# Sink attention's row sums, inverted by another engine

## The chip, the cores and the metric

The program runs on one core of a Trainium2 chip. A core has five engines that each work through a list of their own, in order: TensorE (PE in the profile, with its weight loads as PEld), VectorE (DVE), ScalarE (ACT), GpSimd (POOL) and SyncE (SP, which only starts DMAs here). They meet through semaphores. The metric is the device time of one execution in microseconds.

## What is computed

Attention over 768 positions, for 2 batches and 8 heads of 64 columns, in which each query sees the 4 first positions (the sinks) and a window of 128 positions; then a feed-forward block with a gated convolution; then a mixture of four attention experts. The change lies in the division by the row sums of the first attention:

```python
scores = np.where(keep, scores, -1000000000.0)
scores = scores - np.max(scores, axis=-1, keepdims=True)
a = np.exp(scores)
a = a / (np.sum(a, axis=-1, keepdims=True) + 1e-09)
return np.matmul(a, v).astype(np.float32)
```

## The kernel before, in words

The first attention (span 0 to about 150 us) works on tiles of 128 queries: 6 tiles for each of 2 batches, 12 in all. Each tile runs in 4 steps, one for each pair of heads. In a step `a1_S` multiplies queries by keys (TensorE, L500 for the first batch and L487 for the second), subtracts from the mask and takes the row maximum (VectorE, L502), and takes exponentials whose row sums land in two columns of a small tile `su` (ScalarE, L505, each with a second instruction that reads the sum out). After its 4 steps a tile has `su`, 128 queries by 8 heads. `a1_r` adds the epsilon (L512) and inverts (L513), in place. `a1_rT` lets TensorE transpose `su` to 8 by 128 (L530); the result `rT` is copied from PSUM by ScalarE or VectorE (L517, L519), written to DRAM (L534) and read back spread over the partitions as `R` (L541). `x_norm` multiplies the attention's output by it (L545).

Around this, TensorE transposes the exponentials (`a1_T`, L561) and multiplies them by the values (`a1_V`, L603). GpSimd collects the sinks' columns into `G` (`a1_gather`, L576 for each pair, L578 for each tile), computes two slices of `vsr`, the low part of the sinks' values, in the first batch (L308), and from about 60 us, when the feed-forward block starts to overlap with the second batch, does a multiplication by a convolution weight (L792, tile `ht`) and the low part of the gate (L820, tile `g`) for each step of that block. VectorE and ScalarE also decode the 64-bit weights in the background (L355 to L365, tile `f64u`; L429, L523, L525).

Everything is written in Python in the order in which each engine is to do it (`manual_schedule`). The order comes from time steps: each part of a tile has a lag in steps (`LAGS`), and within a step the string `ORD1` sets the sequence. In it `a1.gather`, `a1.S` and `a1.r` (the second batch) stand in the middle and `a0.r` (the first batch) stands near the end. `a1_r` runs one step behind its tile's last `a1_S`; `a1_rT` one or more parts later. An engine never passes over an instruction that waits: whatever stands behind it in that engine's list waits too.

Of the kernel before, what the change touches and what calls it, by code (L numbers as in the profile page):

```python
# [8 lines left out]
F32 = mybir.dt.float32  # L9
# [6 lines left out]
ALU = mybir.AluOpType  # L16
# [3 lines left out]
B, H, S, D = 2, 8, 768, 64  # L20
P = 128
# [19 lines left out]
EPS = 1e-9  # L41
# [6 lines left out]
def run_phases(phases):  # L48


    at = {}
    for k, (o, n, stages, rate) in enumerate(phases):
        for m, (lag, fn, *g) in enumerate(stages):
            for i in range(n):
                first = i - i % g[0] if g else i
                at.setdefault(o + math.floor(lag + first * rate), []).append((k, m, i, fn))
    for t in sorted(at):
        for _, _, i, fn in sorted(at[t], key=lambda c: c[:3]):
            fn(i)
# [30 lines left out]
class Kernel:  # L90
# [57 lines left out]
    def consts(self, pool):  # L148
        nc = self.nc
        self.words = pool.tile([P, 4], I32, name="words")  # L150
        self.ident = pool.tile([P, P], F32, name="ident")
        self.causal = pool.tile([P, 4 * P], F32, name="causal")
        self.cw = pool.tile([P, 3 * NF], F32, name="cw")
        self.flag = pool.tile([P, 1], I32, name="flag")
        self.lims = pool.tile([P, 2], F32, name="lims")
        self.guard = pool.tile([P, 2 * NF + 1], F32, name="guard")
        self.ones = pool.tile([P, 1], F32, name="ones")
        self.below = pool.tile([P, 1], F32, name="below")
        self.nsink, self.window = self.lims[:, 0:1], self.lims[:, 1:2]
        self.m0 = pool.tile([P, P], F32, name="m0")  # L160
        self.m1 = pool.tile([P, 2 * P], F32, name="m1")
        self.mEO = [pool.tile([P, 2, KW], F32, name=f"m{i}x") for i in range(2)]
# [346 lines left out]

    def a1_r(self, b, qt):  # L510
        r = self.a1s[(b, qt)]
        self.nc.vector.tensor_scalar(r, r, EPS, None, op0=ALU.add)  # L512
        self.nc.vector.reciprocal(r, r)  # L513

    def copy(self, e, dst, src):
        if e == "a":
# [661 lines left out]
    def program(self, general):  # L1178
        tc, nc = self.tc, self.nc
        tg = "g" if general else "f"  # L1180
        self.x, self.y, self.v2, self.lg, self.rw = {}, {}, {}, {}, {}
        self.ks, self.qs = {}, {}
        self.qkv, self.wraw, self.a2P, self.a2PT, self.a2z = {}, {}, {}, {}, {}
        with ExitStack() as ctx:
            def op(name, bufs=1, **kw):
                g = tc.tile_pool(name=name + tg, bufs=bufs, reuse_waits="tile", **kw)
                return g, g.__enter__()

            self.halves = not general
            gSm, self.pSm = op("small", bufs=6)  # L1190
            gR, self.pR = op("R", bufs=15)
            gK, self.pK = op("K")
            gW, self.pW = op("W", bufs=18)
            if general:
                gPS, self.pPS = op("psumg", space=PSUM)
                self.nB = 4
                gG, pG = op("gen")
                self.attn_general(pG)
                gG.__exit__(None, None, None)
                gPS.__exit__(None, None, None)  # L1200
            gD, self.pD = op("dram", space=bass.MemoryType.DRAM)
            gPS, self.pPS = op("psum", space=PSUM)
            self.nB = 8
            gWo, pWo = op("wout")
            gWi, pWi = op("win", side="right")
            self.pRaw = pWi
            self.win = tuple(pWi.tile([P, NF, NKC, P], F32R, name=f"win{s}{tg}") for s in "hl")
            self.wout = tuple(pWo.tile([P, NF, NKC, P], F32R, name=f"wout{s}{tg}") for s in "hl")
            (cs, cl), (ws, wl) = self.conv_steps(), self.weight_steps()
            self.bg, self.first_loads, self.credit = cs + ws, (cl, wl), 0  # L1210
            self.ready, self.tails, self.later, self.qlater, self.drip = set(), [], [], [], []
            self.a1P, self.a1s, self.a1L, self.a1Pg, self.a1PT, self.a1SPT, self.a1G, self.a1O = {}, {}, {}, {}, {}, {}, {}, {}
            if general:
                for f in self.first_loads:
                    f()
                for w in (self.win, self.wout):
                    for f in range(NF):
                        self.need(w, f)
            else:
                self.warm()  # L1220

                self.qbuf = [self.Rt([P, NPAIR, 2, P], F32, "q") for _ in range(2)]
                for i, q in enumerate(self.qbuf):
                    (nc.vector if i == 0 else nc.gpsimd).memset(q[:D, :, 1, :], 0.0)
                    (nc.vector if i == 0 else nc.gpsimd).memset(q[D:, :, 0, :], 0.0)
                nc.sync.dma_start(self.words, self.lim)
                for n, lo, hi in (("k", 0, 1), ("q", 0, 1), ("k", 1, 2), ("q", 1, 2), ("v", 0, 2), ("bg", 0, 1),
                                  ("k", 2, 4), ("bg", 1, 2), ("v", 2, 3)):
                    if n == "bg":
                        self.first_loads[lo]()  # L1230
                    else:
                        self.load_qkv(0, n, lo, hi)
                    if (n, lo) == ("q", 0):
                        nc.scalar.activation(self.sm(1, "e"), self.zeros[:, :1], AF.Exp)
                self.indices()
                self.limits()
                self.masks()
                self.fixed()
                first = [self.attn_phase(b, b * NSTEP, LAGS[b], self.attn_misc(b)) for b in range(B)]
                m1 = NSTEP + MLP_START  # L1240

            def swap_in(i):
                if i == 0:
                    gWi.__exit__(None, None, None)
                    self.gA, self.pA = op("A2", side="right")

            def swap_out(i):
                if i == 3:
                    gWo.__exit__(None, None, None)
                    self.gP2, self.pP2 = op("P2")  # L1250
                    self.wo_ = tuple(self.pP2.tile([P, NP2, DM], F32R, name=f"wo{s}{tg}") for s in "hl")
                if i in (5, 6):
                    p = i - 5
                    raw = self.Wt([P, DM], s="raw")
                    nc.sync.dma_start(raw, self.wo[p * P : (p + 1) * P, :])
                    self.wraw[p] = (raw, self.wo_[0][:, p, :], self.wo_[1][:, p, :])
                if i in (8, 9):
                    self.hilo(*self.wraw.pop(i - 8))

            if general:  # L1260
                first, m1 = [], 0
            m, n, z, t = self.mlp_phase(m1)
            q0 = self.qkv_phase(0, t)
            swap = [(t, q0[1], [(0, f)], 1) for f in (swap_in, swap_out)]
            t1 = t + q0[1]
            q1 = self.qkv_phase(1, t1)
            c0 = self.a2_phase(0, t + A2_START[0])
            c1 = self.a2_phase(1, max(t + A2_START[0] + NT * NP2, t1 + A2_START[1]))
            late = (0, t1 + 60, [(0, lambda i: self.run_later())], 1)
            scaled = c1("norm")  # L1270
            if general:
                ph = [m("rest gate"), n("rest"), m("conv H"), n("H gate conv"), late, m("Y"), n("Y"), z("misc more")]
            else:
                a0, a1 = first
                src = {"a0": a0, "a1": a1, "m": m, "n": n, "z": z, "late": late}
                ph = self.order(ORD1, src)
            qlo = (t, t1 + 60, [(0, lambda i: self.run_qlater())], 1)
            src = {"c0": c0, "c1": c1, "q1": q1, "qlo": qlo, "q0": q0, "in": swap[0], "out": swap[1]}
            run_phases([scaled] + ph + self.order(ORD2, src))
            for g in (self.gP2, self.gA, gPS, gD, gW, gK, gR, gSm):  # L1280
                g.__exit__(None, None, None)
# [67 lines left out]
```

## Time and profile before

| | |
|---|---|
| median of 3 runs | 369.08 us (369.08 to 369.60) |
| the profiled execution | 369.49 us, of which the span of its instructions is 367.6 us |
| TensorE busy | 357.8 us, 97% of the span, 2974 matmuls |
| VectorE busy | 272.5 us, 74% |
| ScalarE busy | 257.7 us, 70% |
| GpSimd busy | 91.5 us, 25% |
| TensorE's granted clock | full speed in all 40 slices |

The profile lists single instructions with start and duration, what an engine waited for, and the chain of waits that ended last. A matmul's end is modelled, so a stretch in which TensorE is busy throughout can hide some slack. A weight load's idle time is no loss while the matmul ahead still streams; idle time before a MATMUL row is.

### The profile page before, as it was taken

To read this page: it belongs to the slowest core of one execution; us is meant where nothing else is said; L and a number is where in the kernel's file an instruction comes from. 1 tells how busy PE (TensorE), PEld (TensorE's weight loads), DVE (VectorE), ACT (ScalarE), POOL (GpSimd) and SP (SyncE) were. 2 spreads that over 40 slices of the span, in tenths; PEclk is the share of its full clock that TensorE was granted. 3 is DMA by queue.
4 is the path that set the end of the run, shared out by engine and by line. 5 is a ranking of instruction groups with operands and counts; after the bars stand their busy time and mean duration, and the time that the engine had idled before them with its cause. 6 is when DMAs were issued, how large, how long until landed. Compare 5 with 4: busy or idle time off the path is not lost.

```text
span 367.6 us, 8436 instructions
## 1 busy us (share of the span) xinstructions
PE 357.8 (97%) x2974; PEld 330.5 (90%) x2974; DVE 272.5 (74%) x862; ACT 257.7 (70%) x728; POOL 91.5 (25%) x198
## 2 busy tenths in 40 slices
PE   8999999999999999999999999999999999999994
PEld 5687877899889999999999999999999999988983
DVE  5689899989887996858746587158669687678831
ACT  5799998766886766646546566259778787848841
POOL 7024111244342253520000003000024244505410
PEclk9999999999999999999999999999999999999999
DMA  7965775354331310000021101000000010101112
GB/s 172 307 172 160 232 231 176 116 188 129 112 117 62 116 30 30 4 27 2 1 86 49 37 3 57 3 0 2 2 1 4 18 40 3 58 2 60 57 55 72
DMA packets 20578, 27.49 MB, mean 75 GB/s; under 512 B 2128, under 2 KB 12464, under 8 KB 20528
## 3 DMA queue, kind: packets, MB, share of 16 engines
q1 hardware_dynamic: 19552, 26.35, 22.8%
q10 hardware_dynamic: 976, 0.52, 0.7%
q8 instruction: 25, 0.41, 0.5%
q14 instruction: 25, 0.20, 0.2%
HBM read 23.68 MB, written 3.19 MB: 73 GB/s over the span
## 4 chain that ended last, share of the span: by engine, by line
PE 75%; DVE 12%; ACT 5%; DMA 3%; issue 2%; SPq 1%; POOL 0%; ACTq 0%; DVEq 0%
PE psB L836 15%; PE psB L782 13%; PE psB L1006 9%; PE psB L1098 5%; PE psB L1122 5%; PE psB L937 5%; PE psB L1146 5%; PE psB L603 3%; PE psB L561 3%; PE psB L500 3%; PE psB L1069 3%; PE psB L1068 3%; DVE P L502 2%; DMA raw<-in_w_in_dram 2%; PE psB L487 2%
## 5 line engine op out<-in xcount | busy, mean ns | idle before, releaser
L836 PE MATMUL psB<-g,wouthf 128*128 128x256 f32 (+1 forms) x320 | 68.2, 304 | 0.1
L505 ACT ACTIVATE P<-P,nm 128x260 f32<-128x260 f32 (+2 forms) x96 | 46.4, 485 | 10.4 <-DVE nm L502 10.3
L836 PEld LDWEIGHTS psB<-g,wouthf 128*128 128x128 f32 x320 | 52.7, 188 | 0.7 <-DVE g L820 0.4
L1086 POOL TENSOR_SCALAR P<-P,r 128x256 f32<-128x256 f32 (+5 forms) x48 | 30.3, 644 | 87.2 <-DVE lg L947 38.7
L836 PE MATMUL psB<-g,woutlf 128*128 128x256 f32 (+1 forms) x160 | 48.5, 303 | 0.0
L1075 ACT ACTIVATE P<-P,nm 128x256 f32<-128x256 f32 (+5 forms) x48 | 32.1, 670 | 12.7 <-DVE nm L1074 6.9
L782 PE MATMUL psB<-x,winhf 128*128 128x386 f32 x128 | 33.2, 340 | 0.0
L792 POOL TENSOR_SCALAR ht<-ht,cw 128x256 f32<-128x256 f32 x24 | 16.4, 682 | 67.1 <-ACT ht L788 63.5
L1071 DVE CUSTOM_DVE_ANT_0 P<-psB,causal 128x384 f32<-128x384 f32 (+3 forms) x64 | 30.2, 502 | 2.6 <-PE psB L1069 2.0
L836 PEld LDWEIGHTS psB<-g,woutlf 128*128 128x128 f32 x160 | 30.1, 188 | 0.0
L561 PE MATMUL psB<-ident,P 128*128 128x128 f32 x176 | 29.4, 282 | 0.4 <-POOL snk L223 0.3
L782 PE MATMUL psB<-xh,winhf 128*128 128x258 f32 x96 | 29.3, 305 | 0.1
L782 PE MATMUL psB<-xh,winlf 128*128 128x258 f32 x96 | 27.1, 283 | 0.0
L1006 PE MATMUL psB<-yh,wqh 128*128 128x256 f32 x96 | 27.1, 283 | 0.0
L782 PE MATMUL psB<-xl,winhf 128*128 128x258 f32 x96 | 27.1, 282 | 0.0
L1006 PE MATMUL psB<-yh,wql 128*128 128x256 f32 x96 | 27.0, 282 | 0.0
L1006 PE MATMUL psB<-yl,wqh 128*128 128x256 f32 x96 | 27.0, 281 | 0.0
L517 ACT COPY PT<-psB 128x512 f32<-128x512 f32 (+1 forms) x48 | 25.5, 532 | 0.4 <-PE psB L561 0.4
L500 PE MATMUL psB<-k,q 128*128 128x260 f32 (+2 forms) x96 | 23.6, 368 | 0.8 <-DMA q<-in_q_dram 0.8
L561 PEld LDWEIGHTS psB<-ident,P 128*128 128x128 f32 x176 | 19.6, 141 | 5.1 <-ACT P L505 1.7
L603 PE MATMUL psB<-PT,v 128*64 128x128 f32 x352 | 23.4, 278 | 0.3 <-ACT PT L517 0.3
L603 PEld LDWEIGHTS psB<-PT,v 128*64 128x64 f32 x352 | 18.8, 136 | 5.0 <-issue 2.4
(198 smaller groups left out, 1004.9 us busy)
## 6 DMA issues: line engine op xcount, KB each, us to landing
raw<-in_w_in_dram SPq DMA_DIRECT2D x8, 512.0 KB, 6.7
raw<-in_w_out_dram SPq DMA_DIRECT2D x8, 512.0 KB, 3.3
v<-in_v_dram SPq DMA_DIRECT2D x12, 256.0 KB, 3.5
R<-rD SPq DMA_DIRECT2D x24, 128.0 KB, 3.1
out_dram<-ot SPq DMA_DIRECT2D x11, 256.0 KB, 2.0
k<-in_k_dram SPq DMA_DIRECT2D x9, 260.0 KB
q<-in_q_dram SPq DMA_DIRECT2D x6, 256.0 KB, 3.3
q<-in_q_dram SPq DMA_DIRECT2D x8, 128.0 KB, 3.1
```

The source lines that it names most:

```text
L500: nc.tensor.matmul(dst, t["q", qt][:, pr, j, :], rhs, start=True, stop=True)
L505: nc.scalar.activation(Pt[:, j, :N], Pt[:, j, :N], AF.Exp, bias=nmx[:, j : j + 1], scale=-1.0, accum_out=sums[:, j : j + 1])
L517: self.nc.scalar.copy(dst, src)
L561: nc.tensor.transpose(ps[:, j, c, :], Pt[:, j, c0 : c0 + P], self.ident)
L603: nc.tensor.matmul(o[j * D : (j + 1) * D, pr, :], t["v", kt][:, h * D : (h + 1) * D], PT[:, j, c, :], start=(pr == 0 and c == 0), stop=(qt ...
L782: nc.tensor.matmul(ps[:, : n + 2], w[:, f, kc, :], x[kc], start=(i == 0), stop=(i == len(ops) - 1))
L836: nc.tensor.matmul(self.m1y[d // per][:, d % per, :], w[:, f, d, :], g[k], start=(first and i == 0 and d % per == 0), stop=(last and i == ...
L937: nc.tensor.matmul(ps[:, :NVG], y[:, kc, ts_], w[2][:, kc], start=(i == 0), stop=(i == len(ops) - 1))
L1006: nc.tensor.matmul(ps, w[which][:, kc, cols], y[:, kc, :], start=(i == 0), stop=(i == len(ops) - 1))
L1071: nc.vector.tensor_tensor_reduce(out=Pt[:, lo:hi], in0=ps[:, : hi - lo], in1=mask, scale=-1.0, scalar=BIG, op0=ALU.add, op1=ALU.min, accum ...
L1075: nc.scalar.activation(Pt[:, :N], Pt[:, :N], AF.Exp, bias=nm[:, 0:1], scale=-1.0, accum_out=sums[:, j : j + 1])
L1086: nc.gpsimd.tensor_scalar(Ps[j][:, :N], Ps[j][:, :N], r[:, j : j + 1], 1.0, op0=ALU.mult, op1=ALU.mult)
```

## The change

GpSimd does `a1_r` in place of VectorE: the epsilon is added by the same kind of instruction on the other engine, and the reciprocal becomes an element-wise power with a constant tile `minus` of 128 by 8 values of -1. The tile is set once at the start. No lag and no sequence changes. All later lines move down by one or two.

```diff
+        self.minus = pool.tile([P, H], F32, name="minus")
...
     def a1_r(self, b, qt):
         r = self.a1s[(b, qt)]
-        self.nc.vector.tensor_scalar(r, r, EPS, None, op0=ALU.add)
-        self.nc.vector.reciprocal(r, r)
+        self.nc.gpsimd.tensor_scalar(r, r, EPS, None, op0=ALU.add)
+        self.nc.gpsimd.tensor_tensor(r, r, self.minus, op=ALU.pow)
...
+                nc.gpsimd.memset(self.minus, -1.0)
```

GpSimd's list at the third tile of the first batch (`su_351` in the change). Before:

```order
L576 COPY G_408<-P_412 128x2x2x2 [waits Activation_49]
L308 TENSOR_TENSOR vsr_467<-vs_323,vsr_467 32x512 [waits DMAHW5_49,Activation_49,Pool_49]
L576 COPY G_408<-P_450 128x2x2x2 [waits Pool_49]
L578 COPY G_408<-G_408 128x96 [waits Pool_49]
L308 TENSOR_TENSOR vsr_467<-vs_323,vsr_467 32x512 [waits Pool_49]
```

The same place in the change:

```order
L577 COPY G_410<-P_414 128x2x2x2 [waits Activation_49]
L309 TENSOR_TENSOR vsr_469<-vs_325,vsr_469 32x512 [waits DMAHW5_49,Activation_49,Pool_49]
L513 TENSOR_SCALAR su_351<-su_351 128x8 [waits Pool_49]
L514 TENSOR_TENSOR su_351<-su_351,minus 128x8 [waits Pool_49]
L577 COPY G_410<-P_452 128x2x2x2
L579 COPY G_410<-G_410 128x96 [waits Pool_49]
L309 TENSOR_TENSOR vsr_469<-vs_325,vsr_469 32x512 [waits Pool_49]
```

The two new instructions stand behind the first half of `vsr`, which itself waits for ScalarE and a DMA, and ahead of the tile's last gather.

GpSimd's list at the eighth tile (the second batch's second). Before:

```order
L792 TENSOR_SCALAR ht_1131<-ht_1131,cw 128x256 [waits Activation_49]
L792 TENSOR_SCALAR ht_1172<-ht_1172,cw 128x256 [waits DMAHW4_49,DMAHW7_49,DMAHW0_49,Activation_49]
L820 TENSOR_TENSOR g_1176<-ht_1067,g_1176 128x256 [waits DMAHW2_49,PE_49,Activation_49]
L525 TENSOR_SCALAR wouthf<-f64u_1106 128x512 [waits DVE_49]
```

In the change:

```order
L793 TENSOR_SCALAR ht_1133<-ht_1133,cw 128x256 [waits Activation_49]
L793 TENSOR_SCALAR ht_1174<-ht_1174,cw 128x256 [waits DMAHW4_49,DMAHW7_49,DMAHW0_49,Activation_49]
L513 TENSOR_SCALAR su_999<-su_999 128x8
L514 TENSOR_TENSOR su_999<-su_999,minus 128x8 [waits Pool_49]
L821 TENSOR_TENSOR g_1178<-ht_1069,g_1178 128x256 [waits DMAHW2_49,PE_49,Activation_49]
L526 TENSOR_SCALAR wouthf<-f64u_1108 128x512 [waits DVE_49]
```

Here they stand between the third `ht` and the first `g`. In VectorE's list the two rows of each tile are gone and nothing else moves.

## Rows read from the trace of the kernel before

**Rows 1.** The page: busy us and share; TensorE's busy tenths; the chain's shares.

```profile
PE 357.8 (97%) x2974; PEld 330.5 (90%) x2974; DVE 272.5 (74%) x862; ACT 257.7 (70%) x728; POOL 91.5 (25%) x198
...
PE   8999999999999999999999999999999999999994
...
PE 75%; DVE 12%; ACT 5%; DMA 3%; issue 2%; SPq 1%; POOL 0%; ACTq 0%; DVEq 0%
```

**Rows 2.** VectorE's two instructions: duration ns min/median/max, first and last start.

```profile
L512 DVE TENSOR_SCALAR su<-su x12: 161/164/285, 12.0 to 148.8; 128x8 f32<-128x8 f32 x12
L513 DVE RECIPROCAL su<-su x12: 202/202/203, 12.2 to 149.0; 128x8 f32<-128x8 f32 x12
```

**Rows 3.** TensorE's waits, 0 to 170 us: total us, times, longest.

```profile
PE psB L530 <- DVE su L513: 1.3, 3, 0.8
...
PE psB L611 <- DVE SPT L590: 0.3, 1, 0.3
PE psB L603 <- ACT PT L517: 0.3, 1, 0.3
```

**Rows 4.** Timeline at L530, tiles 4, 6, 7, 8: start us, us, instruction, [idle before].

```profile
36.71 0.27 PE L530 MATMUL psB<-ident,su 128*8 128x128 f32 x1 [0.26 <-DVE su L513]
...
52.10 0.49 PE L487 MATMUL psB<-k,q 64*128 64x128 f32 x4
...
52.69 0.27 PE L530 MATMUL psB<-ident,su 128*8 128x128 f32 x1
...
58.79 0.27 PE L530 MATMUL psB<-ident,su 128*8 128x128 f32 x1 [0.30 <-DVE su L513]
...
71.61 0.27 PE L530 MATMUL psB<-ident,su 128*8 128x128 f32 x1 [0.76 <-DVE su L513]
```

**Rows 5.** Timeline around the third tile's transpose.

```profile
27.10 1.27 POOL L308 TENSOR_TENSOR vsr<-vs,vsr 32x512 fp32r<-32x512 f32 x1 [2.56 <-issue]
...
27.95 0.27 PE L530 MATMUL psB<-ident,su 128*8 128x128 f32 x1
...
28.44 0.19 POOL L576 COPY G<-P 128x8 f32<-128x8 f32 x1
...
28.69 0.26 POOL L578 COPY G<-G 128x96 f32<-128x96 f32 x1
...
29.14 1.45 DVE L359 TENSOR_SCALAR f64u<-f64u 128x512 int32<-128x512 int32 x1 [0.55 <-ACT f64u L355]
...
29.99 0.24 ACT L517 COPY rT<-psB 8x128 f32<-8x128 f32 x1
...
30.51 0.41 DVE L502 CUSTOM_DVE_ANT_0 P<-psB,m1x 128x260 f32<-128x260 f32 x1
```

**Rows 6.** Timeline: GpSimd's instructions after the sums of tiles 4 and 6, the last sum of tile 7.

```profile
34.86 0.19 POOL L576 COPY G<-P 128x8 f32<-128x8 f32 x1 [2.32 <-ACT P L505]
...
51.03 0.19 POOL L576 COPY G<-P 128x8 f32<-128x8 f32 x1 [1.55 <-ACT P L505]
...
57.14 0.19 ACT L505 ACTIVATION_READ_ACCUMULATOR P<-P,nm 128x1 f32 x1
```

**Rows 7.** Timeline: what stands ahead of the new instructions at tiles 8, 9 and 12.

```profile
69.53 1.07 POOL L792 TENSOR_SCALAR ht<-ht,cw 128x256 f32<-128x256 f32 x1 [2.10 <-ACT ht L788]
...
91.89 0.26 POOL L578 COPY G<-G 128x96 f32<-128x96 f32 x1
...
95.83 0.27 PE L530 MATMUL psB<-ident,su 128*8 128x128 f32 x1
...
151.05 0.54 POOL L578 COPY G<-G 128x96 f32<-128x96 f32 x1
...
152.37 0.27 PE L530 MATMUL psB<-ident,su 128*8 128x128 f32 x1
```

**Rows 8.** GpSimd groups by form up to 60 us: count | busy us, mean ns.

```profile
L222 POOL TENSOR_SCALAR pen<-rel,lims 128x128 f32<-128x128 int32 x1 | 0.8, 813 | 0.3 <-DVE lims L172 0.3
```

**Rows 9.** VectorE's line L359: duration ns min/median/max.

```profile
L359 DVE TENSOR_SCALAR f64u<-f64u x17: 179/426/1450, 10.7 to 130.6; 128x512 int32<-128x512 int32 x16, 128x24 int32<-128x24 int32 x1
```

## The prediction

> **What bounds the kernel now.** I read the page first. TensorE is busy for 357.8 of 367.6 us, in nine tenths or more of nearly every slice, and the chain that ended last runs over it for 75% of the span, over VectorE for 12% and over GpSimd for nothing [rows 1]. So an edit matters here by what it does to TensorE's list. The view of who waited for whom then shows that up to 170 us TensorE's largest wait after the start is the very one that the change touches: L530, the transpose of the row sums, waits for VectorE's reciprocal for 1.3 us in 3 pieces [rows 3]. The timeline has the pieces: 0.26 us at tile 4, 0.30 at tile 7, 0.76 at tile 8, and about 0.10 at tile 6, where the matmul ahead ended at 52.59 and the transpose began at 52.69 [rows 4]. That makes 1.42 us. (Tile 1 has a small gap too; the start is set by loads, and I leave it out.) The sums were ready earlier in each case; VectorE came late because it works its own list in order.
>
> **What is removed.** 12 additions of 0.16 us and 12 reciprocals of 0.20 us leave VectorE, 12 x 0.37 = 4.4 us [rows 2]. VectorE is not the bound, so this is worth at most what TensorE waited for it, the 1.42 us above. The list of instructions shows that the two rows per tile do go from VectorE to GpSimd; that the change does nothing is excluded.
>
> **What is added: the price of the power.** No power stands in the trace, so p, the time of one 128x8 power on GpSimd, is bounded by rows. From below: a GpSimd copy of the same 128x8 takes 0.19 us [rows 5], and no power can be less. From above, the longest GpSimd row nearby, the 32x512 subtraction, takes 1.27 us [rows 5]; but it is no real ceiling, since a power is a long series of elementary steps for each element and the other rows are one or two. The row nearest in kind is the one with the most work per element, two steps on 128 integer columns in 0.81 us [rows 8], or 3.2 ns a step and column. A start of 0.19 us and 8 columns at 3.2 ns leave room for 24 steps in 0.8 us. I take p = 0.8 us, an estimate from these rows, and keep 0.19 and 1.27 for the range, with a tail above. The addition I price as the copy, 0.19; between two dependent GpSimd instructions lie 0.06 us (28.44 + 0.19 to 28.69 [rows 5]); and from the power's end to the transpose I allow 0.10. From the moment that GpSimd can begin, the transpose may begin 0.05 + 0.19 + 0.06 + p + 0.10 = 0.40 + p later, 1.20 us.
>
> A rule of the Trainium skill speaks against such a move: "GPSIMD Engine Reference", section "Engine selection", sends element-wise work to VectorE and calls GpSimd about twice as slow for two inputs. It has no price for a power; twice VectorE's pair would be 0.73 us in place of my 0.19 + 0.06 + 0.8 = 1.05, 0.32 less at each of tiles 3, 8 and 12 below, and the result some +0.2 in place of +1.2. No run here shows which.
>
> **Tile by tile.** What matters is where GpSimd's list lets the pair begin.
> Tile 3: it stands behind the first half of `vsr`, which ends at 28.37 [rows 5], while the transpose ran at 27.95 without waiting. It now runs at 28.37 + 1.20 = 29.57, so TensorE is 1.62 us late; in general 0.82 + p. This is the largest term and there is some of it at any p.
> Tiles 4 and 6: the sums are there when GpSimd's gather started, 34.86 and 51.03 [rows 6]. The transposes could run from 36.06 and 52.23, before TensorE asks for them (36.45 and 52.59). Both gaps go: -0.26 and -0.10. In general this holds to p of about 1.2.
> Tile 7: the last sum ends at 57.33 [rows 6], GpSimd is idle; ready at 58.53 where TensorE was free at 58.49. The gap of 0.30 shrinks to 0.04: -0.26.
> Tile 8: behind the third `ht`, which ends at 70.60 [rows 7]; ready at 71.80 against 71.61 before [rows 4]: +0.19.
> Tiles 1, 2 and 5: GpSimd is idle when the sums are done, and TensorE comes later: nothing.
> Tiles 9 to 11: like tile 9, where the gather of the tile ends at 92.15 and the transpose comes at 95.83 [rows 7], with over 2 us to spare: nothing. What stands behind the pair there, the low part of the gate, is wanted by TensorE a step later, so it is hidden too.
> Tile 12: the gather ends at 151.59 and the transpose came at 152.37 [rows 7]; now 152.79: +0.42.
> Sum: 1.62 - 0.26 - 0.10 - 0.26 + 0.19 + 0.42 = +1.6 us.
> Not all of a delay need last. TensorE also waits 0.34 us for L611 and 0.34 for L603, shown as 0.3 each [rows 3], for work that may be on time when TensorE is late, and a stretch that is busy throughout can hide slack, as the ends are modelled. After tile 3 ScalarE wants the transpose's result only at 29.99 and VectorE the next scores at 30.51 [rows 5], so the first 1.6 us of delay reach neither at once. I take off 0.4: **+1.2 us**. On the profiled execution's 369.49 us that is 370.7; its excess of 0.41 over the median is the profiled run's own, so against the median it is 369.08 + 1.2 = 370.3 us.
>
> **The shared path of VectorE and GpSimd.** L359 took 1.45 us once where its median is 0.43 [rows 9], exactly while the second half of `vsr` ran on GpSimd from 29.03 [rows 5]: VectorE was held until GpSimd had finished. So a power may hold VectorE for p. At tile 3 the power would run from 28.7 to 29.5, so L359 would start at 29.5, ahead of `vsr`'s second half, and end near 29.9 in place of 30.59: no loss there. At the other tiles VectorE has just been freed of 0.37 us. I cost it at nothing, and at up to 0.4 us for tiles 4 and 6 if that cover is gone.
> The Trainium skill states this as a rule ("Advanced Engine Details and Errata", section "GPSIMD Details": GpSimd shares a read and a write interface with VectorE and conflicts with its two-port modes and its instructions with two SBUF inputs). The trace agrees, with the 1.45 us.
>
> **The rivals.**
> *Cheap power, no net change.* At p = 0.19 the terms are +1.01 at tile 3, -0.26, -0.10, -0.30, and 70.60 + 0.59 = 71.19 at tile 8, -0.42, and nothing at tile 12: -0.07, or -0.5 with the 0.4 taken off. Anything up to p of about 0.5 lies within 0.74 us of no change: 368.6 to 369.8. For it speaks that all short GpSimd rows are near 0.19; against it, that none of them is a power.
> *Faster.* The delay at tile 3 is absorbed whole, because nobody needs L530 or the matmuls behind it before 29.99, and p is small: then only the gains are left, -0.26 - 0.10 - 0.30 - 0.42 = -1.1, 368.0 us. It needs p under about 0.4 and over 1 us of hidden slack in a stretch where TensorE shows none, so I hold it for unlikely.
> *Heavy power.* GpSimd works the power element by element and p is several us. From p of about 2.2 even tiles with a long lead stall. At p = 3: 3.8 at tile 3, 1.6, 1.7, 2.0 and 2.4 at tiles 4, 6, 7, 8, 2.6 at tile 12, and some 3 at the others: about +17, 386 us. The trace says nothing against it but that the operation's neighbours are short.
>
> **How the numbers follow.** A change of under 0.2%, 0.74 us, is about what a measurement of this kernel can't tell from none. Forecast (p from 0.6 to 1.6, +0.7 to +5): 52%. No net change: 25%. Faster: 11%. Heavy: 12%. At the upper row bound, p = 1.27, the sum is 2.09 - 0.2 + 0.2 + 0.66 + 0.89 = +3.6, 372.7; at p = 1.6 it is near +5, 374.1. The range runs from the faster case's end, 368.2, to 374.3, and leaves out the heavy case and little more. Slower 0.64, same 0.25, faster 0.11.
>
> **What would show it.** Right: the waits of TensorE show L530 held by GpSimd, not VectorE, at tile 3 for 1 to 2 us, and little at tiles 4 and 6; the power's row lies between 0.5 and 1.6 us; L530 of tile 12 waits. Wrong: a power near 0.2 us, or of several us; TensorE late at tile 3 and on time again by 36 us (the delay was absorbed); VectorE's rows stretched beside the powers and TensorE waiting for them (the shared path cost something).

## The result, and the profile after

| | before | after |
|---|---|---|
| median | 369.31 us (369.08 to 369.83, 6 runs) | 374.02 us (373.32 to 375.43, 6 runs) |
| ratio | | 1.013, 95% interval 1.0116 to 1.0144 |
| span of the profiled execution | 367.6 us | 372.2 us |
| VectorE / GpSimd busy | 272.5 / 91.5 us | 269.2 / 116.9 us |

The change is slower by 4.7 us, or 1.3%. The forecast was +1.2 us, with a range up to 374.3. A second set of runs beside the later experiments gave 373.77 against 369.15, the same +4.6.

The page of the kernel after, busy time and the chain's shares, as in [rows 1]:

```profile
PE 357.6 (96%) x2974; PEld 330.8 (89%) x2974; DVE 269.2 (72%) x838; ACT 258.0 (69%) x728; POOL 116.9 (31%) x223
...
PE 72%; DVE 9%; ACT 6%; POOL 4%; DMA 4%; issue 3%; SPq 1%; ACTq 0%; DVEq 0%; POOLq 0%
```

TensorE has the same work (357.6 us against 357.8) in a span that is 4.6 us longer, so it stood idle for longer. GpSimd, which had no part in the chain, now has 4%.

The groups of GpSimd's two new instructions, by line: count, then busy us and mean ns, idle before; then their durations, min/median/max:

```profile
L514 POOL TENSOR_TENSOR su<-su,minus 128x8 f32<-128x8 f32 x12 | 21.0, 1753 | 1.0
...
L514 POOL TENSOR_TENSOR su<-su,minus x12: 1658/1668/2103, 10.1 to 155.0; 128x8 f32<-128x8 f32 x12
...
L513 POOL TENSOR_SCALAR su<-su x12: 238/250/407, 9.7 to 154.7; 128x8 f32<-128x8 f32 x12
```

A power of 128x8 takes 1.67 us, against 0.20 for the reciprocal that it replaces [rows 2]. The addition takes 0.25 on GpSimd against 0.16.

TensorE's waits in the stretch 0 to 170 us, total, times, longest, where [rows 3] had 1.3 us in 3 pieces:

```profile
PE psB L531 <- POOL su L514: 6.3, 6, 2.0
```

The timeline gives the six pieces. TensorE at tiles 2, 3, 6, 7, 8 and 12 of the kernel after, as in [rows 4]:

```profile
21.27 0.27 PE L531 MATMUL psB<-ident,su 128*8 128x128 f32 x1 [0.17 <-POOL su L514]
...
31.18 0.27 PE L531 MATMUL psB<-ident,su 128*8 128x128 f32 x1 [2.02 <-POOL su L514]
...
55.82 0.27 PE L531 MATMUL psB<-ident,su 128*8 128x128 f32 x1 [0.50 <-POOL su L514]
...
62.47 0.27 PE L531 MATMUL psB<-ident,su 128*8 128x128 f32 x1 [1.02 <-POOL su L514]
...
75.83 0.27 PE L531 MATMUL psB<-ident,su 128*8 128x128 f32 x1 [1.47 <-POOL su L514]
...
156.96 0.27 PE L531 MATMUL psB<-ident,su 128*8 128x128 f32 x1 [1.12 <-POOL su L514]
```

They sum to 6.3 us; before, tiles 4, 6, 7 and 8 cost 1.42. The difference is 4.9 us, but it is not the same thing as the 4.6 us that the span gained. From the second transpose to the end of the span the change takes 3.6 us more (350.9 against 347.4), so some of the waiting is made good. The other 1.0 us lies ahead of the second transpose, which came at 21.27 against 20.23: 0.17 of it is its own wait, the rest stands behind a weight load that lands at another time in each execution (see "The change again"). GpSimd at the third tile, the counterpart of [rows 5]:

```profile
27.79 1.26 POOL L309 TENSOR_TENSOR vsr<-vs,vsr 32x512 fp32r<-32x512 f32 x1 [2.60 <-issue]
29.13 0.24 POOL L513 TENSOR_SCALAR su<-su 128x8 f32<-128x8 f32 x1
29.45 1.67 POOL L514 TENSOR_TENSOR su<-su,minus 128x8 f32<-128x8 f32 x1
31.07 0.19 POOL L577 COPY G<-P 128x8 f32<-128x8 f32 x1
```

The pair starts 0.08 us after the first half of `vsr` and the transpose follows the power's end (31.12) by 0.06. So from the moment GpSimd is free to the transpose it takes 31.18 - 29.05 = 2.13 us.

### The profile page after: what moved, and what is told of

Same layout as the page of the kernel before. It is cut to its first block, busy times and chain, and to the rows that moved or that the text cites. A ratio compares the mean times of both kernels' runs of the same rounds, so it can differ in the third digit from the quotient of the medians.

```text
span 372.2 us, 8438 instructions
## 1 busy us (share of the span) xinstructions
PE 357.6 (96%) x2974; PEld 330.8 (89%) x2974; DVE 269.2 (72%) x838; ACT 258.0 (69%) x728; POOL 116.9 (31%) x223
## 4 chain that ended last, share of the span: by engine, by line
PE 72%; DVE 9%; ACT 6%; POOL 4%; DMA 4%; issue 3%; SPq 1%; ACTq 0%; DVEq 0%; POOLq 0%
PE psB L837 13%; PE psB L783 13%; PE psB L1007 9%; PE psB L1099 5%; PE psB L1123 5%; PE psB L938 5%; PE psB L1147 5%; PE psB L604 3%; PE psB L1070 3%; PE psB L1069 3%; PE psB L562 2%; POOL su L514 2%; PE psB L501 2%; ACT P L506 2%; DMA raw<-in_w_in_dram 2%
## 5 line engine op out<-in xcount | busy, mean ns | idle before, releaser
L783 PEld LDWEIGHTS psB<-x,winhf 128*128 128x128 f32 x128 | 23.1, 189 | 0.0
```

Source lines behind the costliest of these rows:

```text
L783: nc.tensor.matmul(ps[:, : n + 2], w[:, f, kc, :], x[kc], start=(i == 0), stop=(i == len(ops) - 1))
```

## The experiments

Each run is compared with runs of the kernel before that were measured beside it on the same chip (three sets: 369.31, 369.15 and 369.45 us). Line numbers are those of the run; L529 to L535 is the same transpose.

### A product in place of the power

```diff
-        self.nc.gpsimd.tensor_tensor(r, r, self.minus, op=ALU.pow)
+        self.nc.gpsimd.tensor_tensor(r, r, self.minus, op=ALU.mult)
```

> GpSimd multiplies the sums by -1 in place of the power; everything else is the change (the division by the row sums is thereby left out). Theory 'price' (the loss is the power's own 1.67 us behind which TensorE waits): the product takes about 0.25 us, L531 waits only at tile 3, for about 1.1 us, the waits of before at tiles 4, 6, 7, 8 are gone, and the time is within 0.5 us of before, 368.8 to 369.8. Rival 'engine' (the loss lies in the hand-over to GpSimd, its list, or the interface shared with VectorE, whatever is computed): at least half of the +4.7 us stays, 371.5 or more.

Measured: 370.11 us, ratio 1.0019 (1.0007 to 1.003). The product's durations (min/median/max), and TensorE's waits from 10 to 170 us:

```profile
L514 POOL TENSOR_TENSOR su<-su,minus x12: 202/203/650, 10.1 to 152.1; 128x8 f32<-128x8 f32 x12
...
PE psB L531 <- POOL su L514: 1.3, 2, 0.9
```

The wait is down from 6.3 to 1.3 us, at tiles 3 and 8 alone. The time lies 0.3 us above what "price" expected and far below "engine". Of the +4.7 us about 3.9 belong to the power, and 0.8 (0.3 to 1.1) to the rest of the move. As L531's waits are now about as long as those of before, the 0.8 is not explained by them. Nor does the profile show it: from the second transpose on, this one takes only 0.3 us more than that of before (347.7 against 347.4). Its cause is open.

### The pair ahead of the background step

```diff
-... a0.T a0.misc a1.sL a0.r a1.rT ...
+... a0.T a0.r a0.misc a1.sL a1.rT ...
```

> The change with the first batch's pair issued ahead of the background step, so that at tile 3 it stands in front of the first half of vsr in GpSimd's list. Theory 'place' (the 2.02 us at tile 3 come from standing behind vsr): the pair starts when the sums are there, about 26.7, the power ends near 28.8, TensorE's wait at tile 3 goes, and 1.2 to 2.0 us come back: 372.0 to 372.8. Rival 'absorbed' (the delay of tile 3 was made good later, and other places set the loss): 373.6 or more.

Measured: 371.28 us, ratio 1.0053 (1.0035 to 1.0071): 2.7 us below the change. The third tile, GpSimd and TensorE:

```profile
25.42 0.24 POOL L513 TENSOR_SCALAR su<-su 128x8 f32<-128x8 f32 x1 [1.56 <-ACT P L506]
25.75 2.19 POOL L514 TENSOR_TENSOR su<-su,minus 128x8 f32<-128x8 f32 x1
28.02 1.27 POOL L309 TENSOR_TENSOR vsr<-vs,vsr 32x512 fp32r<-32x512 f32 x1
```

```profile
27.99 0.27 PE L531 MATMUL psB<-ident,su 128*8 128x128 f32 x1 [0.17 <-POOL su L514]
```

The pair starts when ScalarE's sums are there and the wait falls from 2.02 to 0.17 us; tiles 6, 7, 8 and 12 keep theirs (4.5 us over all six pieces). So the third tile's delay came from the place behind `vsr`, and it was not made good later. More came back (2.7, where 1.2 to 2.0 were expected) than the 1.85 us of wait. Runs differ by 0.5 us either way, and the lower clock that can follow the gap of 2.02 us (see "The change again") may be a part; no trace of the other executions shows it.

### The transpose asked for one step later, in the change and in the kernel before

```diff
-LAGS = ((1, 2, 1, 4, 3, 4, 5, 5, 2, 7, 7, 9, 11), (1, 1, 2, 6, 3, 4, 5, 3, 2, 5, 6, 7, 7))
+LAGS = ((1, 2, 1, 4, 3, 4, 5, 5, 3, 7, 7, 9, 11), (1, 1, 2, 6, 3, 4, 5, 4, 3, 5, 6, 7, 7))
```

> The change, with the transpose of the sums asked for one step later in both batches (and R read one step later in the second). Theory 'waits' (the loss is the 6.3 us in which TensorE stands before L531, against 1.5 before): the waits go nearly whole, 368.0 to 369.5. Rival 'shared' (a power holds VectorE's instructions or delays what stands behind it on GpSimd): the waits of L531 go but 1 us or more of the loss stays, 370.5 or more.

> The kernel before with the same later transpose: the control for the run ahead. Theory 'waits': the 1.4 us in which TensorE waited for VectorE's reciprocal go, 367.9 to 368.8, and the difference to the run ahead is under 0.7 us. Rival: the later transpose costs of its own (R late for the product at L545), 369.5 or more.

Measured: 372.40 us (1.0054 to 1.0102) with GpSimd's pair, 371.98 (1.0045 to 1.0095) with VectorE's. TensorE's waits from 10 to 170 us, first with GpSimd's pair, then with VectorE's:

```profile
PE psB L562 <- ACT P L506: 0.9, 3, 0.4
PE psB L612 <- DVE SPT L591: 0.6, 1, 0.6
PE psB L783 <- DVE nm L503: 0.5, 1, 0.5
```

```profile
PE psB L561 <- ACT P L505: 1.7, 4, 1.0
PE psB L611 <- DVE SPT L590: 0.6, 1, 0.6
PE psB L603 <- ACT PT L517: 0.5, 1, 0.5
PE psB L487 <- DVE nm L502: 0.5, 1, 0.5
```

Both expectations of a time near before failed. The first time lies where "shared" put it (370.5 or more), but the control, which has no power, lies there too: the control's rival holds, the later order costs 2.7 us by itself. L531 drops out of the list, and new waits for exponentials and copies take its place. Within the later order the two kernels differ by 0.4 us, inside their intervals, which are about 1 us wide to each side: where TensorE asks late enough, a power of 1.67 us costs nothing that can be measured here. The 2.7 us are only partly shown as waits (the profiled execution of the first was its fastest, 370.57 us); where the rest lies was not pursued.

### The change again

> The change once more, as the measure beside the others of this call. Its first profile had TensorE idle for 0.89 us at 14.3 us, behind a weight load that landed 0.7 us later than in the profile of before. Theory 'waits': the six waits before L531 come back within 0.3 us each (2.0, 0.5, 1.0, 1.5, 1.1 and 0.2), the time is 373.3 to 374.8, and the idle time at 14.3 is that of a load, which differs from run to run. Rival: the idle time at 14.3 is there again at 0.8 us or more, so it belongs to the change.

Measured: 373.77 us, ratio 1.0126 (1.0107 to 1.0146). The wait before L531 is again 6.3 us in 6 pieces, the longest 2.0. The idle time at 14.3, 0.89 us in the first profile, is 0.56 here; it ends when ScalarE has the first weight load, which differs by run. First the kernel before, then the change's second profile, the decoding that waits for that load:

```profile
13.18 0.66 ACT L355 ACTIVATE f64u<-raw 128x512 f32<-128x512 f32 x1 [0.58 <-DMA raw<-in_w_in_dram]
```

```profile
13.37 0.69 ACT L356 ACTIVATE f64u<-raw 128x512 f32<-128x512 f32 x1 [0.95 <-DMA raw<-in_w_in_dram]
```

So single profiles are compared at L531, not by their whole span.

One thing differs that the waits do not show. In the first profile TensorE's granted clock stayed at 1.00 after the 2.02 us before the third transpose. Here the same 2.02 us were followed by 0.50, the lower of the clock's two levels (1.2 of 2.4 GHz). The stretch (us, busy us and instructions of PE, PEld, DVE, ACT and POOL, TensorE's granted clock, DMA share, GB/s):

```profile
31.00:34.00 3.00, 3.00 (x14) 2.14 (x14) 0.92 (x5) 1.44 (x5) 1.67 (x4) 0.50 0.03 8
```

From the third transpose to the fourth the same work took 9.92 us (30.68 to 40.60) in place of 8.30 (31.18 to 39.47). So the gap can cost 1.6 us more than its length. This execution was the slowest of the four, 375.18 us against 373.54 to 373.99; how often the clock falls in executions without a profile is not known.

### Inverting after the transpose

```diff
-        self.nc.vector.tensor_scalar(r, r, EPS, None, op0=ALU.add)
-        self.nc.vector.reciprocal(r, r)
+        pass
...
-        self.copy(ENG_R[b], rT, ps)
+        self.nc.vector.tensor_scalar(rT, ps, EPS, None, op0=ALU.add)
+        self.nc.vector.reciprocal(rT, rT)
```

> The raw sums are transposed at once; VectorE then adds the epsilon on the way out of PSUM (8x128) and inverts there. L530 then waits for no pair on any engine. Theory 'waits': TensorE's 1.4 us at tiles 4, 6, 7 and 8 go, 367.7 to 368.8. Rival 'VectorE': the pair and the first batch's copy now lie on VectorE at other moments and delay what TensorE needs next (L502, L590), 369.3 or more.

Measured: 373.19 us, ratio 1.0111 (1.0093 to 1.013). VectorE's reciprocal in its new shape (min/median/max), and what TensorE waits for from 10 to 170 us:

```profile
L532 DVE RECIPROCAL rT<-rT x12: 940/941/942, 13.0 to 157.9; 8x128 f32<-8x128 f32 x12
```

```profile
PE psB L561 <- ACT P L505: 1.8, 2, 0.9
PE psB L561 <- ACT PT L516: 1.0, 2, 0.6
PE psB L611 <- DVE SPT L590: 0.8, 1, 0.8
PE psB L603 <- ACT PT L516: 0.6, 1, 0.6
```

The rival holds, more strongly than it was put. The same 1024 reciprocals laid out as 8 rows of 128 take 0.94 us in place of 0.20, so VectorE has 7 us more to do (279.7 busy), and TensorE, which no longer waits for the sums, waits for what VectorE and ScalarE deliver late.

### GpSimd only where there is a lead

```diff
+        if (b, qt) in ((0, 0), (0, 4), (1, 2), (1, 3)):
             self.nc.gpsimd.tensor_scalar(r, r, EPS, None, op0=ALU.add)
             self.nc.gpsimd.tensor_tensor(r, r, self.minus, op=ALU.pow)
+        else:
+            self.nc.vector.tensor_scalar(r, r, EPS, None, op0=ALU.add)
+            self.nc.vector.reciprocal(r, r)
```

> Pair on GpSimd, with the power, at tiles 1, 5, 9 and 10 only, where TensorE asked for the sums over 0.4 us after the power; VectorE does the others. Theory 'waits': neither the power nor the relief of VectorE counts there, 368.9 to 369.8. Rival 'shared': each power costs something wherever it stands, a third of 4.7 us, 370.8 or more.

Measured: 369.69 us, ratio 1.0019 (1.0008 to 1.0031), as "waits" expected. Four powers of about 1.7 us cost 0.5 us together (0.3 to 1.1), not the 1.6 of "shared". TensorE's waits for the sums are those of before (1.3 us in 3 pieces), so they don't explain the 0.5, as with the product's 0.8. VectorE's relief at these tiles bought nothing.

### The power by its width

> The change with six extra powers of 128 by 1, 2, 8, 16, 32 and 64 and products of 128 by 8 and 64 on scratch data, on GpSimd while it is idle in the middle of the program; only their rows are wanted. Theory: the power is a loop over columns, about 0.2 us of start and (1.67 - 0.2)/8 = 0.18 us a column, so 0.4, 0.6, 1.7, 3.1, 6.1 and 12 us. Rival: a fixed start (a code path or a table) makes most of the 1.67 us, and 64 columns take under 5 us. VectorE's rows beside the long powers are stretched if GpSimd holds the shared interface during them, and at their medians if not.

This kernel ran once (373.18 us); only its rows are of use. The groups on GpSimd, 170 to 200 us: count, busy us, mean ns. The first six are powers, the last two products:

```profile
L1251 POOL TENSOR_TENSOR probe<-probe,probe 128x64 f32<-128x64 f32 x1 | 10.6, 10551 | 0.1
L1251 POOL TENSOR_TENSOR probe<-probe,probe 128x32 f32<-128x32 f32 x1 | 5.5, 5450 | 0.1
L1251 POOL TENSOR_TENSOR probe<-probe,probe 128x16 f32<-128x16 f32 x1 | 2.9, 2901 | 0.1
L1251 POOL TENSOR_TENSOR probe<-probe,probe 128x8 f32<-128x8 f32 x1 | 2.0, 1969 | 0.1
L1251 POOL TENSOR_TENSOR probe<-probe,probe 128x1 f32<-128x1 f32 x1 | 0.9, 872 | 0.0
...
L1251 POOL TENSOR_TENSOR probe<-probe,probe 128x2 f32<-128x2 f32 x1 | 0.7, 703 | 0.1
L1253 POOL TENSOR_TENSOR probe<-probe,probe 128x64 f32<-128x64 f32 x1 | 0.3, 325 | 0.1
L1253 POOL TENSOR_TENSOR probe<-probe,probe 128x8 f32<-128x8 f32 x1 | 0.2, 205 | 0.1
```

From 32 to 64 columns the power takes 5.10 us more, 0.159 a column; the start is 5.45 - 32 x 0.159 = 0.35 us. The product takes (325 - 205) / 56 = 2.1 ns a column, so a power's column costs 75 times as much. The theory of a loop over columns holds; the widths of 1 and 8 came out longer than the line, and VectorE instructions with two SBUF inputs ran when they began. VectorE's rows beside the longest power are at their medians (0.62 and 0.55 us), but for one that began 0.04 us after it and took 0.70 in place of 0.56. So the power doesn't hold the shared interface throughout.

### The kernel before with its pair ahead

The first edit is that of the second experiment, made in the kernel before. The other adds:

```diff
-... a1.S a1.V a1.sV a1.xl a1.r a0.S ...
+... a1.r a1.S a1.V a1.sV a1.xl a0.S ...
```

> The kernel before (VectorE's pair) with the first batch's pair issued ahead of the background step, so that in VectorE's list it stands in front of the 0.69 us of weight decoding. Theory 'waits': TensorE's waits at tiles 4 and 6 (0.26 and 0.10 us) go and nothing else moves, 368.6 to 369.2, 0 to 0.5 us faster than before. Rival: what VectorE does now comes later by the same 0.37 us and TensorE meets that instead, 369.2 to 370.

> As the run ahead, and in the second batch the pair stands in front of a step's new scores in VectorE's list. Theory 'waits': the waits at tiles 7 and 8 (0.30 and 0.76 us) go too, 367.9 to 368.8. Rival: the scores' maxima come 0.37 us later and TensorE waits for the exponentials (L561) instead, 369.2 or more.

Measured: 368.78 us, ratio 0.998 (0.9966 to 0.9994), and 368.91 us, 0.9984 (0.997 to 0.9998). TensorE's waits from 10 to 170 us with the first batch alone, then with both:

```profile
PE psB L530 <- DVE su L513: 1.1, 2, 0.8
```

```profile
PE psB L561 <- ACT P L505: 1.7, 3, 0.6
...
PE psB L530 <- DVE su L513: 0.2, 1, 0.2
```

The first is some 0.7 us (0.2 to 1.3) faster than before and 5 us faster than the change: the version to keep, if only by 0.2%. Tile 4's wait of 0.26 us is gone, tile 6's is not; the rest of the 0.7 is not explained. In this profile L359 was also not held by GpSimd (0.43 us, against the 1.45 of [rows 9]), which may by itself bring tile 4's sums earlier. In the second profile L359 took 1.49 us again and tile 4 has no wait either, so the order is enough. In the second the wait for the sums goes at tile 7 and falls to 0.16 at tile 8, as "waits" says, and waits for exponentials come in its place, as the rival says; the time lies between the two ranges and nothing more is gained.

### The power twice

```diff
+        self.nc.gpsimd.tensor_tensor(r, r, self.minus, op=ALU.pow)
```

> The change with the power done twice, one behind the other (so the sums are not inverted). Theory 'serial' (each power lies on TensorE's path wherever GpSimd's list leaves it no lead): another 1.75 us at tiles 2, 3, 4, 6, 7, 8, 12, 1.6 at tile 11, about 1 at tiles 1 and 5, 0.2 at tile 9, some 14 to 16 us in all over the change, 386 to 390. Rival 'absorbed' (only the first delays last, the later ones ride on a TensorE that is late anyway): under 382.

Measured: 396.59 us, ratio 1.0723 (1.0687 to 1.0758), 22.6 us over the change and above both expectations. Busy time from the page; TensorE's wait from 0 to 190 us; then stretches, columns as in "The change again", the granted clock third from the end:

```profile
PE 367.9 (93%) x2974; PEld 338.9 (86%) x2974; DVE 268.4 (68%) x838; ACT 260.6 (66%) x728; POOL 133.3 (34%) x235
...
PE psB L532 <- POOL su L515: 18.5, 9, 3.7
...
30.00:34.00 4.00, 0.27 (x2) 0.06 (x2) 1.11 (x5) 1.82 (x7) 3.75 (x5) 0.89 0.64 215
34.00:36.00 2.00, 2.00 (x8) 1.80 (x9) 0.00 (x0) 0.84 (x2) 1.80 (x5) 0.50 0.01 2
...
38.00:41.00 3.00, 3.00 (x19) 2.50 (x16) 1.03 (x4) 1.12 (x4) 0.55 (x1) 0.68 0.18 54
...
66.00:70.00 4.00, 4.00 (x31) 2.83 (x31) 2.38 (x8) 2.54 (x9) 0.35 (x3) 0.66 0.53 169
...
75.00:80.00 5.00, 4.89 (x25) 4.45 (x25) 1.95 (x6) 1.95 (x6) 0.55 (x3) 0.50 0.28 98
...
180.00:184.00 4.00, 4.00 (x25) 3.85 (x25) 2.06 (x5) 1.10 (x3) 2.40 (x4) 0.59 0.20 58
```

The waits rise by 18.5 - 6.3 = 12.2 us, near "serial" (14 to 16); "absorbed" falls. The other 10.3 us are in TensorE's own busy time, 367.9 against 357.6 for the same matmuls. The granted clock falls to 0.50 three times: during the 3.73 us without a matmul before the third transpose, until about 40 us; after 2.22 us before the sixth, from about 67 to 81 us; and after 2.84 us before the twelfth, from about 180 to 183 us. That is some 22 us of work at half the clock, which by estimate costs half of it, 11 us. That term stood in neither theory.

## Why the prediction was right or wrong

*What bounds the kernel.* Right. What the change adds in the profile from the second transpose on is TensorE's idle time before one transpose. No run shows a gain from what VectorE was spared, 4.4 us by its rows (its busy time fell by 3.3).

*The price of the power.* This is the term that was mis-sized: 0.8 us taken, 1.67 measured, above the 1.27 kept as the row bound. The step that failed is the pricing of a step of the power at 3.2 ns a column with room for 24 steps; a column costs 159 ns, 50 such steps. The bound from above was the longest neighbour, and the text said itself that this was no ceiling; a tail to 1.6 us was kept, and its sum is near +5. That 374.02 lies inside the range, 0.3 us below its end, is due to this tail and not to the estimate. It is also in part luck: with 1.67 the same working gives +6.1, or +5.7 with the 0.4 taken off, 1.0 more than was measured. (At 1.27 the sum of +3.6 leaves the 0.4 in, and at 0.6 the terms give +0.6 and not +0.7.)

*The way from GpSimd's free moment to the transpose*, 0.40 + p: 2.07 by formula with the measured power, 2.13 measured at tile 3. The addition was 0.25 and not 0.19; the hand-over 0.06 and not 0.10.

*Tile by tile.* With p = 1.67 the same working gives waits of 0.51 at tile 6, 0.91 at tile 7, 1.82 at tile 8 and 1.29 at tile 12; measured 0.50, 1.02, 1.47 and 1.12. At tile 3 it gives a transpose 2.5 us later than before; measured from the second transpose, it came 2.2 us later (9.91 against 7.72 us). The third tile was named as the largest, and the second experiment confirms place and size. Tile 4 has no wait, as forecast, where the working gives 0.48: its sums came 6.1 us after the third transpose, against 6.9 before, where GpSimd had held L359. That TensorE was late is not the reason, since in the second experiment it was not (36.29 against 36.71) and tile 4 has no wait there either. Tile 2, costed at nothing, waited 0.17, since its power was stretched to 2.10 us.

*What is made good.* 0.4 us was taken off, and about 1.1 us was made good: after the second transpose the waits rose by 4.7 us and the rest of the span by 3.6. The transposes show most of it: the eighth comes at 75.83 against 71.61, 4.2 us late, the ninth 3.2 us late (99.05 against 95.83 [rows 7]). So 1.0 us is regained between them, 0.34 of it L603's wait [rows 3]; the rest is not seen as idle time in the trace of before.

*The clock.* The prediction has no term for it. In the change's second profile it cost 1.6 us, in the first nothing.

*The signs.* The transpose waits for GpSimd at tile 3 (2.02 us, where 1 to 2 were named) and at tile 12. The power, 1.67 us, lies just outside the 0.5 to 1.6 named.

*The shared path.* Costed at nothing, rightly, but for another reason than given; see the last section.

*The rivals.* "Cheap power" is what the product did: 370.11 where that rival said 368.6 to 369.8, so even then the move would have brought nothing. "Faster" needed the delay at tile 3 absorbed, and the second experiment shows that it was not. "Heavy power" is the double power, which cost more than a sum of waits, by the clock. The rule of the Trainium skill that was weighed ("GPSIMD Engine Reference", section "Engine selection", about twice VectorE's time) would have put the pair at 0.73 us; it measured 1.99 to the power's end, 0.24 + 0.08 + 1.67. The rule speaks of adding, multiplying and taking a maximum. The addition took 0.25 us on GpSimd and 0.16 on VectorE, 1.5 times; the power took eight times VectorE's reciprocal, and the rule does not cover it.

## What to carry to other kernels

Before an operation moves to an idle engine, look for that operation's own price there: rows of other operations don't bound it, and a row of the same shape was wrong here by a factor of eight. Then read, for each place, what stands ahead in the new engine's list and when the bound engine asks: four powers with a lead cost 0.5 us together, one behind a 1.27 us subtraction cost about 2. To remove a wait of the bound engine, first try the order in the old engine's list; that took 0.7 us off where the move added 4.7. And count a wait of TensorE as able to cost more than its length: the same 2.02 us were followed by the lower clock in one profile and not in the other.

## What the runs showed of the hardware

*A power on GpSimd* takes about 0.35 us and 0.159 us for each column of 128 partitions (the run by width, 32 to 64 columns), a product 2.1 ns a column.

*A long GpSimd instruction need not hold VectorE.* In the trace of before a 1.27 us subtraction held L359 for about 1 us [rows 5, 9]. Beside the powers nothing of the kind is seen. VectorE in the kernel after, first the same decoding step (now L360) during the third tile's power (29.45 to 31.12), then an instruction with two SBUF inputs during the eighth tile's (74.11 to 75.78):

```profile
29.81 0.43 DVE L360 TENSOR_SCALAR f64u<-f64u 128x512 int32<-128x512 int32 x1 [0.18 <-ACT f64u L356]
...
74.66 0.48 DVE L800 SCALAR_TENSOR_TENSOR ht<-ht,cw 128x256 f32<-128x256 f32 x1
```

They take 0.43 and 0.48 us, their medians. Where one of the two gave way in this trace and in the second experiment's, it was the power: it took 2.10 us at tile 2 and 2.19 in the second experiment, in both cases beside a VectorE instruction with two SBUF inputs (L366, 0.69 us) that was running when it began. The product at tile 2 was held in the same way, 0.65 us against 0.20. "Advanced Engine Details and Errata" of the Trainium skill, section "GPSIMD Details", names the shared interface and the conflict; these rows agree with a conflict over accesses, of which a power would have few, and not with one that lasts as long as the instruction. That reading is argued from the rows; no run was made to test it.

*The clock.* The length of a gap alone does not tell whether the lower level follows. The change's 2.02 us without a matmul left the clock at 1.00 in its first profile and were followed by 0.50 in its second. In the double power's run it fell during 3.73 us and after 2.22 and 2.84 us, but not with 3.38 us, from 89.5 to 92.9. Stretches of that run around this gap, columns as above:

```profile
89.00:93.00 4.00, 0.62 (x9) 0.43 (x9) 3.09 (x8) 2.91 (x9) 3.84 (x4) 1.00 0.14 34
93.00:97.00 4.00, 4.00 (x39) 3.87 (x40) 2.28 (x8) 2.19 (x7) 2.33 (x7) 1.00 0.26 101
```

TensorE is busy for 0.62 of the first 4 us and the clock stays at 1.00. What else decides was not pursued.
